# Holding the stationary operand over four segments and over two output halves in a fused attention and gMLP kernel

## The chip, the cores and the metric

The kernel runs on one core of a Trainium2 chip. The metric is the device time of one execution in microseconds.

## The reference

Two blocks with residuals over x of 2048 tokens by 1024 features: a segmented attention with memory (32 heads, 4 segments of 512 tokens), then a gMLP. The change touches only the gMLP:

```python
z  = gelu(einsum('bsd,df->bsf', x, w_in))            # 1024 -> 3584
z1 = z[..., :1792]                                   # the "first half": the first changed stage
z2 = layernorm(z[..., 1792:])
g  = einsum('ts,bsf->btf', w_sp, z2) + b_sp          # mixes tokens
return einsum('bsf,fd->bsd', z1 * g, w_out)          # output projection: the second changed stage
```

## The kernel before

Operations are recorded per engine and the waits are derived from what they read and write. A matmul computes `dst += lhs.T @ rhs`: `lhs` (128x128) is the stationary operand, loaded into the array by a weight load of its own, and `rhs` (here up to 512 columns) streams past it. The results gather in PSUM, of which the kernel uses eight banks; "evacuating" a bank is reading its result out. Every matmul call of this kernel makes a weight load and a matmul.

```python
def mm8(dst, lhs, rhs, n=8):                # one PSUM bank: n matmuls, n loads
    for i in range(n):
        pe.matmul(dst, lhs(i), rhs(i), start=(i == 0), stop=(i == n - 1))
# ... (attention; the second gMLP half; eight PSUM banks in turn from here on)

# first gMLP half: 14 output chunks fc, 4 segments s, 8 matmuls each
for k in range(4, 8):
    # ...
    for fl in range(w // 128):
        fc = lo // 128 + fl
        for s in range(NSEG):
            b = next_bank()
            mm8(bank(b), lambda i: WIN[k % 3][:, i, fl * 128:(fl + 1) * 128], lambda i: HNT[s][:, i, :])
            act.activation(Z1T[:, fc, s * 512:(s + 1) * 512], bank(b), ACTF.Gelu_apprx_tanh)
            if zq:
                z2_apply()
    # ... (loads of the next slabs)

for tb in range(4):
    # ... (token mixing: 14 banks of 16 matmuls into YT, evacuated by DVE)
    for tcl in range(4):                    # output projection: 16 chunks tc of 128 tokens
        tc = 4 * tb + tcl
        fin = FIN[tc % 3]
        sp.dma_start(fin[:], out2d[tc * 128:(tc + 1) * 128, :])
        for lo, w in ((0, 512), (512, 512)) if tc < NTC - 1 else ((0, 512), (512, 384), (896, 128)):
            b = next_bank()
            hs = slice(lo, lo + w)
            mm8(PS[:, b, 0:w], lambda i: YT[:, i, tcl * 128:(tcl + 1) * 128], lambda i: WOUT[:, i, hs], n=14)
            dve.tensor_tensor(fin[:, hs], fin[:, hs], PS[:, b, 0:w], ALU.add)
            sp.dma_start(out2d[tc * 128:(tc + 1) * 128, hs], fin[:, hs])
```

In the first half the stationary operand `WIN[.., i, ..]` does not depend on `s`, so it is loaded four times; in the output projection `YT[:, i, ..]` does not depend on the column half, so it is loaded twice.

The softmax here doesn't subtract the row's maximum and nothing guards it: scores larger than these inputs give would overflow.

## Time and profile before

| | before |
|---|---|
| time, median | 796.79 us (796.41 to 797.04, 3 runs) |
| span of the profiled run | 795.1 us |
| matmuls, weight loads | 5657, 5657 |
| PE busy, weight loads busy | 99%, 48% |
| first gMLP half | 405.6 to 502.3 us, 448 matmuls |
| output projection | four blocks between 550.9 and 793 us, 462 matmuls |
| start to start of the matmuls there, 512 columns | 215.8 ns |

The head of the profile's page, before. PE is TensorE's matmuls, PEld its weight loads (LDWEIGHTS), which overlap the matmuls, DVE is VectorE, ACT ScalarE, POOL GpSimd; the numbers are busy time, share of the span and count.

```profile
span 795.1 us, 13111 instructions
PE 789.9 (99%) x5657; PEld 378.4 (48%) x5657; DVE 379.3 (48%) x745; ACT 295.6 (37%) x347; POOL 172.1 (22%) x329
```

The groups of instructions of the changed stages, before: busy time in us and mean ns of one; after the second bar, idle time of the engine ahead of them.

```profile
L209 PE MATMUL ps<-w_out,yT 128*128 128x512 bf16 (+2 forms) x462 | 97.4, 373 | 0.0
L209 PE MATMUL ps<-hnT,win 128*128 128x512 bf16 x448 | 96.9, 379 | 0.0
L209 PEld LDWEIGHTS ps<-w_out,yT 128*128 128x128 bf16 x462 | 44.7, 98 | 52.3
L209 PEld LDWEIGHTS ps<-hnT,win 128*128 128x128 bf16 x448 | 43.8, 98 | 52.8
```

Two things are to be read here. A matmul's record lasts 379 ns, but 448 of them fill only 96.9 us: they overlap, and 96.9 us / 448 = 216 ns is the pace. And a load's 98 ns look like 45% of that pace. The starts of single instructions in the trace, from 410.142 us on, in ns (worked out from the trace's start times):

```text
410142 matmul   410144 load
410358 matmul   410360 load
410574 matmul   410576 load
```

Each load, for the next matmul, starts 1 or 2 ns after the start of the running one and ends 98 ns later, more than 100 ns before it is wanted. The starts also tell what is not streaming: 215.8 ns at 512 columns and 55.8 at 128 (in the last chunk) differ by 160 ns / 384 = 0.4167 ns per column, so 512 columns are 213.3 ns and 2.5 ns are left over. The windows of the changed stages, before (busy time of each engine in the window, count in brackets, then granted clock, DMA share, GB/s):

```profile
405.60:502.30 96.70, 96.70 (x450) 43.83 (x448) 10.88 (x21) 33.38 (x56) 5.65 (x15) 1.00 0.16 39
550.90:795.00 244.10, 241.90 (x1135) 110.34 (x1133) 81.67 (x119) 0.00 (x0) 0.00 (x0) 1.00 0.22 53
```

PE is busy for all of the first stage; ACT, which evacuates it, for a third.

### The profile page before, as it was taken

How to read it: one execution, taken by the hardware profiler on the slowest of the kernel's cores; microseconds unless marked ns; L12 is line 12 of the kernel's file. 1: busy time of each engine (PE TensorE's matmuls, PEld its weight loads, DVE VectorE, ACT ScalarE, POOL GpSimd, SP SyncE). 2: the span in 40 equal slices, each digit the busy share in tenths (PEclk: the TensorE clock that was granted, in tenths of full speed). 3: DMA queues.
4: the chain of work that ended last, by engine and by line, in shares of the span. 5: the costliest groups of instructions: out<-in, count | busy, mean ns of one | idle time of the engine just before them, and what ended most of it. 6: DMA issues, size and time to landing. Idle time of an engine off the chain costs nothing.

```text
span 795.1 us, 13111 instructions
## 1 busy us (share of the span) xinstructions
PE 789.9 (99%) x5657; PEld 378.4 (48%) x5657; DVE 379.3 (48%) x745; ACT 295.6 (37%) x347; POOL 172.1 (22%) x329
## 2 busy tenths in 40 slices
PE   8999999999999999999999999999999999999998
PEld 3445455554554455455544444444444444444444
DVE  7664689679854766744562000053234323323332
ACT  5777877887787675133333333100000000000000
POOL 4564565565553331100230000000000000000000
DMA  9862555363415325411116000740270043011002
GB/s 292 181 162 57 94 81 121 87 105 84 107 23 125 114 67 139 121 47 54 54 54 132 1 1 0 222 90 7 79 133 1 33 109 78 1 59 54 1 7 86
DMA packets 125002, 64.83 MB, mean 82 GB/s; under 512 B 94992, under 2 KB 113936, under 8 KB 124944
## 3 DMA queue, kind: packets, MB, share of 16 engines
q1 hardware_dynamic: 124944, 63.99, 33.7%
q8 instruction: 44, 0.72, 0.4%
q14 instruction: 14, 0.11, 0.1%
HBM read 32.51 MB, written 8.39 MB: 51 GB/s over the span
## 4 chain that ended last, share of the span: by engine, by line
PE 96%; DMA 2%; DVE 1%; ACT 0%; SPq 0%; issue 0%
PE ps L209 96%; DMA wq<-in_A_wq_dram 2%; DMA xch<-in_A_x_dram 0%; DVE stats L209 0%; ACT junk L209 0%; DVE xnT L209 0%; DVE lno L209 0%; SPq L209 0%; ACT xnT L209 0%; DVE mv L209 0%; DVE fin L209 0%
## 5 line engine op out<-in xcount | busy, mean ns | idle before, releaser
L209 PE MATMUL ps<-wspT,z 128*128 128x512 bf16 x896 | 194.0, 379 | 0.0
L209 ACT ACTIVATE e<-ps 128x2048 bf16<-128x2048 f32 (+1 forms) x96 | 152.6, 1590 | 41.9 <-PE ps L209 41.8
L209 PEld LDWEIGHTS ps<-wspT,z 128*128 128x128 bf16 x896 | 87.7, 98 | 105.7
L209 DVE TENSOR_TENSOR tmpg<-ps,brow 128x512 f32<-128x512 f32 x56 | 38.7, 691 | 196.7 <-DMA brow<-in_B_b_sp_dram 104.0
L209 POOL TENSOR_SCALAR_AFFINE_SELECT e<-e 128x512 bf16<-128x512 bf16 x128 | 90.4, 718 | 127.2 <-ACT e L209 127.1
L209 PE MATMUL ps<-win,hnT 128*128 128x448 bf16 x512 | 98.3, 352 | 0.0
L209 PE MATMUL ps<-w_out,yT 128*128 128x512 bf16 (+2 forms) x462 | 97.4, 373 | 0.0
L209 PE MATMUL ps<-hnT,win 128*128 128x512 bf16 x448 | 96.9, 379 | 0.0
L209 PEld LDWEIGHTS ps<-win,hnT 128*128 128x128 bf16 x512 | 49.7, 98 | 46.4 <-issue 0.2
L209 PEld LDWEIGHTS ps<-w_out,yT 128*128 128x128 bf16 x462 | 44.7, 98 | 52.3
L209 PEld LDWEIGHTS ps<-hnT,win 128*128 128x128 bf16 x448 | 43.8, 98 | 52.8
L209 PE MATMUL ps<-xnT,wk 128*128 128x512 bf16 x256 | 60.8, 380 | 0.0
L209 PE MATMUL ps<-xnT,wq 128*128 128x512 bf16 x256 | 60.6, 379 | 0.1
L209 PE MATMUL ps<-wv,xnT 128*128 128x512 bf16 x256 | 59.4, 380 | 0.2 <-ACT xnT L209 0.2
L209 ACT ACTIVATE z<-ps 128x448 bf16<-128x448 f32 x60 | 32.5, 543 | 69.4 <-PE ps L209 69.4
L209 PE MATMUL ps<-wo,oT 128*128 128x512 bf16 x256 | 58.0, 379 | 0.0
L209 ACT ACTIVATE z1T<-ps 128x512 bf16<-128x512 f32 x56 | 33.4, 597 | 63.3 <-PE ps L209 63.3
L209 DVE TENSOR_TENSOR fin<-fin,ps 128x512 bf16<-128x512 bf16 (+2 forms) x33 | 22.2, 671 | 71.2 <-DMA fin<-out_dram 39.7
L209 DVE BATCH_NORM_STATS2 zst<-z 128x6 f32<-128x448 bf16 x64 | 38.9, 619 | 30.1 <-ACT z L209 30.1
L209 PEld LDWEIGHTS ps<-v,e 128*128 128x128 bf16 x1280 | 38.8, 96 | 14.0 <-issue 6.5
L209 PE MATMUL ps<-v,e 128*128 128x33 bf16 x1280 | 42.2, 178 | 0.0
L209 DVE TENSOR_TENSOR yT<-tmpg,z1T 128x512 bf16<-128x512 f32 x56 | 38.8, 692 | 1.9
(86 smaller groups left out, 609.3 us busy)
## 6 DMA issues: line engine op xcount, KB each, us to landing
xch<-in_A_x_dram SPq DMA_DIRECT2D x16, 256.0 KB, 3.3
xr<-in_A_x_dram SPq DMA_DIRECT2D x16, 256.0 KB, 3.7
out_dram<-hch SPq DMA_DIRECT2D x16, 256.0 KB, 2.4
fin<-out_dram SPq DMA_DIRECT2D x16, 256.0 KB, 2.8
out_dram<-fin SPq DMA_DIRECT2D x31, 128.0 KB, 1.7
win<-in_B_w_in_dram SPq DMA_DIRECT2D x4, 896.0 KB, 5.1
w_out<-in_B_w_out_dram SPq DMA_DIRECT2D x1, 3584.0 KB, 12.7
win<-in_B_w_in_dram SPq DMA_DIRECT2D x3, 1024.0 KB, 5.2
```

The lines of the kernel that those rows point to most:

```text
L209: ins = getattr(e, op.name)(*op.args, **op.kw)
```

## The change

The intent: products with the same stationary operand run back to back and load it once. In the first half the four segments are computed together in four PSUM banks; in the output projection the two column halves in two banks (the last chunk, split in three parts, stays as it was). A held matmul is one that is issued without a weight load.

```diff
+def held_matmul(e, out, lhsT, rhs, start, stop):
+    return e.add_instruction(mybir.InstMatmult(
+        ..., tile_size=(128, 128), tile_position=(0, 0), ldweights=False,
+        ins=[e.lower_ap(rhs), e.lower_ap(lhsT)], outs=[e.lower_ap(out)]))
 ...
+    def mm_held(dsts, lhs, rhss, n):
+        for i in range(n):
+            for k, (d, r) in enumerate(zip(dsts, rhss)):
+                (pe.matmul_held if k else pe.matmul)(d, lhs(i), r(i), start=(i == 0), stop=(i == n - 1))
 ...
+            bs = [next_bank() for _ in range(NSEG)]
+            mm_held([bank(b) for b in bs], lambda i: WIN[k % 3][:, i, fl * 128:(fl + 1) * 128],
+                    [lambda i, s=s: HNT[s][:, i, :] for s in range(NSEG)], 8)
             for s in range(NSEG):
-                b = next_bank()
-                mm8(bank(b), lambda i: WIN[k % 3][:, i, fl * 128:(fl + 1) * 128], lambda i: HNT[s][:, i, :])
-                act.activation(Z1T[:, fc, s * 512:(s + 1) * 512], bank(b), ACTF.Gelu_apprx_tanh)
+                act.activation(Z1T[:, fc, s * 512:(s + 1) * 512], bank(bs[s]), ACTF.Gelu_apprx_tanh)
 ...
+            parts = ((0, 512), (512, 512)) if tc < NTC - 1 else ((0, 512), (512, 384), (896, 128))
+            bs = [next_bank() for _ in parts]
+            if tc < NTC - 1:
+                mm_held([bank(b) for b in bs], lambda i: YT[:, i, tcl * 128:(tcl + 1) * 128],
+                        [lambda i, lo=lo, w=w: WOUT[:, i, lo:lo + w] for lo, w in parts], 14)
+            for (lo, w), b in zip(parts, bs):
 ... (additions and stores as before, now after both halves)
```

("..." marks what is left out.)

More of the change, by code (lines that the diff above doesn't have):

```diff
@@ L26 @@
 GRAN = 32
+def held_matmul(e, out, lhsT, rhs, start, stop):
+    return e.add_instruction(mybir.InstMatmult(
+        name=e.bass.get_next_instruction_name(), engine=mybir.EngineType.PE, start_tensor_calc=start,
+        stop_tensor_calc=stop, tile_size=(128, 128), tile_position=(0, 0), ldweights=False,
+        ins=[e.lower_ap(rhs), e.lower_ap(lhsT)], outs=[e.lower_ap(out)]))
 class _Op:
@@ L208, in run @@
                     e.wait_ge(o.dma if o.dma is not None else sems[o.eng], o.val)
-                ins = getattr(e, op.name)(*op.args, **op.kw)
+                if op.name == "matmul_held":
+                    ins = held_matmul(e, *op.args, **op.kw)
+                else:
+                    ins = getattr(e, op.name)(*op.args, **op.kw)
                 if op.dma is not None:
@@ L912, in bass_sequential_preLN__memory_aug_infini_attn__mixer_gmlp__prompt_kernel @@
             sp.dma_start(fin[:], out2d[tc * 128:(tc + 1) * 128, :])
-            for lo, w in ((0, 512), (512, 512)) if tc < NTC - 1 else ((0, 512), (512, 384), (896, 128)):
-                b = next_bank()
+            parts = ((0, 512), (512, 512)) if tc < NTC - 1 else ((0, 512), (512, 384), (896, 128))
[4 more added lines that the diff above has]
+            for (lo, w), b in zip(parts, bs):
                 hs = slice(lo, lo + w)
-                mm8(PS[:, b, 0:w], lambda i: YT[:, i, tcl * 128:(tcl + 1) * 128], lambda i: WOUT[:, i, hs], n=14)
+                if tc == NTC - 1:
+                    mm8(PS[:, b, 0:w], lambda i: YT[:, i, tcl * 128:(tcl + 1) * 128], lambda i: WOUT[:, i, hs], n=14)
                 dve.tensor_tensor(fin[:, hs], fin[:, hs], PS[:, b, 0:w], ALU.add)
```

## The prediction

> **What bounds the kernel.** TensorE. The page gives PE 99% of a 795.1 us span, the chain of waits 96% PE, and the list of waits shows PE waiting for other engines only 2.7 us in all, none of it after 400 us, where both changed stages lie. The granted clock is 1.000.
>
> **The two stages.** By the windows, the first gMLP half runs from 405.6 to 502.3 us (448 matmuls, 128x512) and the output projection (462 matmuls) is spread in four blocks over 550.9 to 793 us. Every matmul has its own weight load (5657 of each); one load takes 98 ns. In the trace, start to start of the matmuls in both stages is 215.8 ns, while the load of the next operand starts 2 ns after each matmul's start. 512 columns at 2.4 GHz are 213.3 ns, so 2.5 ns per matmul are not streaming. The Trainium skill (TensorE: Matmul & The Clock Gate, "Step-by-step") says that loads are pulled ahead of running matmuls into a background buffer; this trace agrees. The same page ("Wait — 56ns, not 53.3ns?") calls the 2.5 ns a fixed cost per matmul; the trace agrees that it is fixed: 448 columns take 189.2 ns (186.7 + 2.5) and 128 columns 55.8 ns (53.3 + 2.5).
>
> **What the change does.** It removes 336 weight loads (three of four in 448) and 210 (15 chunks x 14), 546 in all: 53.5 us of weight-load busy time, all of it under running matmuls, so none of it on the critical path. It moves evacuations: four gelus (0.60 us each) now come in a burst after 32 matmuls (6.9 us), on banks 0-3 and 4-7 in turn; the burst (about 2.4 us) has 6.9 us. In the output projection two additions (0.69 us) follow 28 matmuls (6.04 us); also free. Alternating banks costs nothing where the kernel already does it (the early V projection: 216 ns).
>
> **On the critical path.** Only the 2.5 ns could go, if it were the change of weights and not the matmul itself: 546 x 2.5 ns = 1.4 us at most, 0.2%. I think it more likely (about 60 to 40) that it stays. At the tail, both additions of the chunk before the last now come after its 28 matmuls, so the last load of fin is issued about 0.7 us later. Before, 0.73 us of idle time followed the addition that waits for that load (790.63 us); the shift just fits: 0 to 0.2 us.
>
> **Prediction.** 796.3 us, 8 in 10 between 794.8 and 797.4. Faster by over 2%: 1%; within 2%: 98%; slower by over 2%: 1%.
>
> **What would show it.** Weight loads 5111, PEld busy 378 down to about 325 us, about 41% of the span; PE busy still 99%; start to start of held matmuls 215.8 ns (or 213.3 if the swap was the cost); no new PE waits in the two stages; the first half's window still 96.7 us (95.9 if the swap was the cost); DVE no longer waiting on fin in the output projection.
>
> **What would make it wrong.** A held matmul that costs more than one with its own load (for instance, a load after held matmuls that is not pulled ahead: up to 98 ns x 322 loads (112 + 210) = 32 us, 4% slower); a lower granted clock; a semaphore wait that now falls on the first matmul of a group of four banks.

## The result, and the profile after

| | before | after |
|---|---|---|
| time, median | 796.91 us (796.41 to 797.15, 4 runs, one more than above) | 796.97 us (796.54 to 797.23, 4 runs) |
| ratio | | 1.0001, 95% interval 0.9984 to 1.0018 |
| weight loads | 5657 | 5111 |
| weight loads busy | 378.4 us | 325.6 us |
| span of the profiled run | 795.1 us | 795.2 us |

A ratio here and below is the mean time of one kernel's fast runs over that of the other's fast runs of the same rounds, so it is not quite the ratio of the medians. The time did not move.

The head of the page, after, and the groups of the changed stages. L31 is the line of the held matmul.

```profile
span 795.2 us, 12473 instructions
PE 785.4 (99%) x5565; PEld 325.6 (41%) x5111; DVE 378.1 (48%) x745; ACT 291.0 (37%) x347; POOL 173.5 (22%) x329
...
L31 PE MATMUL ps<-hnT,win 128*128 128x512 bf16 x332 | 90.6, 379 | 0.5
L220 PE MATMUL ps<-w_out,yT 128*128 128x512 bf16 (+2 forms) x243 | 82.4, 367 | 0.0
L31 PE MATMUL ps<-w_out,yT 128*128 128x512 bf16 x210 | 79.6, 379 | 0.5
...
L220 PEld LDWEIGHTS ps<-w_out,yT 128*128 128x128 bf16 x252 | 24.2, 98 | 72.2 <-issue 69.1
...
L220 PEld LDWEIGHTS ps<-hnT,win 128*128 128x128 bf16 x112 | 11.0, 98 | 85.0 <-issue 84.9
```

The loads went as meant: 448 to 112 and 462 to 252. The 92 matmuls that seem to be gone (5565 of 5657) are missing records, not missing work: in the first half the start times are 215 or 216 ns apart but for eight gaps of 431 or 432 ns, twice that, each where one record is missing; token mixing has 18 such gaps and the output projection nine. With those set aside the pace is 215.8 ns, as before, for held matmuls and for those with a load. The load of the next operand starts 1 or 2 ns after the start of the last held matmul of a group (matmul at 410.891 us, load at 410.892). The windows, after:

```profile
405.60:502.30 96.70, 96.22 (x441) 11.00 (x113) 10.94 (x21) 27.51 (x54) 5.71 (x15) 1.00 0.17 38
550.90:795.00 244.10, 240.84 (x1114) 89.82 (x923) 80.13 (x119) 0.00 (x0) 0.00 (x0) 1.00 0.22 53
```

In the first window PEld fell from 43.83 to 11.00 us, while the stage is as long as it was: 96.48 us from the start of its first matmul to that of its last (405.83 to 502.30 before, 405.93 to 502.40 after; after, the first record is missing, and its start is set one step before the second's). The output projection takes 241.71 us by the same measure, before and after.

ACT's 5.9 us less in that window are not work saved in the stage's bottleneck. 1.3 us of them are evacuations that now fall behind the window's end (ACT has 1.94 us in the window after it, 0.60 before); the other 4.5 come from the new order. The evacuations in order of time, before and after (start in us, length, instruction, idle time ahead of it and what ended it):

```profile
488.91 0.60 ACT L209 ACTIVATE z1T<-ps 128x512 bf16<-128x512 f32 x1 [1.13 <-PE ps L209]
490.63 0.60 ACT L209 ACTIVATE z1T<-ps 128x512 bf16<-128x512 f32 x1 [1.13 <-PE ps L209]
492.36 0.60 ACT L209 ACTIVATE z1T<-ps 128x512 bf16<-128x512 f32 x1 [1.13 <-PE ps L209]
494.09 0.60 ACT L209 ACTIVATE z1T<-ps 128x512 bf16<-128x512 f32 x1 [1.13 <-PE ps L209]
```

```profile
488.36 2.06 ACT L220 ACTIVATE z1T<-ps 128x512 bf16<-128x512 f32 x4 [4.84 <-PE ps L220]
495.27 2.06 ACT L220 ACTIVATE z1T<-ps 128x512 bf16<-128x512 f32 x4 [4.84 <-PE ps L220]
```

Four gelus in a row overlap and take 2.06 us, not four times 0.60 us. ACT waits for PE in both kernels, so this gains nothing.

The tail, before and after: DVE's last additions, and the queue's issue of the last load of fin (the buffer with the rows of the output to which a product is added).

```profile
787.90 0.38 SPq L209 DMA_DIRECT2D fin<-out_dram  x1
790.63 0.69 DVE L209 TENSOR_TENSOR fin<-fin,ps 128x512 bf16<-128x512 bf16 x1 [3.19 <-DMA fin<-out_dram]
792.05 0.55 DVE L209 TENSOR_TENSOR fin<-fin,ps 128x384 bf16<-128x384 bf16 x1 [0.73 <-PE ps L209]
792.83 0.29 DVE L209 TENSOR_TENSOR fin<-fin,ps 128x128 bf16<-128x128 bf16 x1 [0.23 <-PE ps L209]
```

```profile
788.46 0.38 SPq L220 DMA_DIRECT2D fin<-out_dram  x1
791.32 1.39 DVE L220 TENSOR_TENSOR fin<-fin,ps 128x512 bf16<-128x512 bf16 x2 [3.32 <-DMA fin<-out_dram]
792.93 0.29 DVE L220 TENSOR_TENSOR fin<-fin,ps 128x128 bf16<-128x128 bf16 x1 [0.23 <-PE ps L220]
```

The load is issued 0.56 us later and the addition that waits for it starts 0.69 us later. It runs into the next one (the "x2" of 1.39 us), which had 0.73 us of idle time ahead of it before; the last addition still starts 0.23 us after DVE fell idle, released by PE. The delay was swallowed whole. The 0.10 us between the two last lines was there already when the last matmul started (792.577 us before, 792.678 after), and already at the first matmul of the second gMLP half, ahead of both changed stages (291.837 and 291.938).

### The profile page after: what moved, and what is told of

It is laid out like the page before. It is cut to its first block, busy times and chain, and to the rows that moved or that the text cites. A ratio compares the mean times of both kernels' runs of the same rounds, so it can differ in the third digit from the quotient of the medians.

```text
span 795.2 us, 12473 instructions
## 1 busy us (share of the span) xinstructions
PE 785.4 (99%) x5565; PEld 325.6 (41%) x5111; DVE 378.1 (48%) x745; ACT 291.0 (37%) x347; POOL 173.5 (22%) x329
## 4 chain that ended last, share of the span: by engine, by line
PE 94%; DVE 5%; issue 1%; ACT 0%; DVEq 0%
PE ps L220 79%; PE ps L31 15%; DVE stats L220 1%; DVE hch L220 1%; DVE otok L220 0%; DVE lno L220 0%; DVE pqk L220 0%; DVE ta L220 0%; ACT e L220 0%; DVE etmp L220 0%; DVE rd L220 0%; DVE mv L220 0%; DVE rdm L220 0%; DVE upd L220 0%; DVE xnT L220 0%
## 5 line engine op out<-in xcount | busy, mean ns | idle before, releaser
L31 PE MATMUL ps<-hnT,win 128*128 128x512 bf16 x332 | 90.6, 379 | 0.5
L220 PE MATMUL ps<-w_out,yT 128*128 128x512 bf16 (+2 forms) x243 | 82.4, 367 | 0.0
L31 PE MATMUL ps<-w_out,yT 128*128 128x512 bf16 x210 | 79.6, 379 | 0.5
L220 PE MATMUL ps<-xnT,wq 128*128 128x512 bf16 x225 | 53.9, 379 | 1.8 <-issue 0.2
L220 ACT ACTIVATE z1T<-ps 128x512 bf16<-128x512 f32 x56 | 28.9, 603 | 68.7 <-PE ps L220 68.7
L220 PEld LDWEIGHTS ps<-w_out,yT 128*128 128x128 bf16 x252 | 24.2, 98 | 72.2 <-issue 69.1
L220 PEld LDWEIGHTS ps<-hnT,win 128*128 128x128 bf16 x112 | 11.0, 98 | 85.0 <-issue 84.9
```

What stands on the lines that cost most here:

```text
L31: return e.add_instruction(mybir.InstMatmult(name=e.bass.get_next_instruction_name(), engine=mybir.EngineType.PE, start_tensor_calc=start, ...
L220: ins = getattr(e, op.name)(*op.args, **op.kw)
```

## The experiments

The theory: loads are wholly hidden under the matmuls, and the 2.5 ns by which a matmul of 512 columns exceeds its 213.3 ns of streaming belong to the matmul. Two rivals also give an unchanged time: the loads saved did gain and the new order of banks and evacuations cost as much (rival 1), or one stage gained and the other lost (rival 2). The first four runs shared a chip, and 7 runs of the kernel before (median 796.69 us).

### order_only: the new order with every load

```diff
-                (pe.matmul_held if k else pe.matmul)(d, lhs(i), r(i), start=(i == 0), stop=(i == n - 1))
+                pe.matmul(d, lhs(i), r(i), start=(i == 0), stop=(i == n - 1))
```

> The new order of matmuls and evacuations, but every matmul with its own weight load (5657 loads). Theory (loads are wholly hidden, and the 2.5 ns over streaming belong to the matmul, not to the load): start to start 215.8 ns in both stages, the time of before within 0.1%, ratio 1.000. Rival 1 (the removed loads gained up to 546 x 2.5 ns = 1.4 us and the new order of banks and evacuations costs as much): this kernel pays the order without the gain, about 798.3 us, ratio about 1.002, with a start to start above 216 or a wait of PE in one of the two stages.

Measured: 796.56 us, ratio 0.9997 (0.9982 to 1.0012), 5657 loads, start to start 215.8 ns in both stages, and no wait of PE in either. The bursts of four gelus in 2.06 us are there too, so ACT's saved time comes from the order and not from the loads. The order costs nothing; rival 1 falls.

### z1_only and out_only: one half of the change each

```diff
 z1_only: the output projection is that of the kernel before
-            if tc < NTC - 1:
-                mm_held([bank(b) for b in bs], ... 14)
+                mm8(PS[:, b, 0:w], ... n=14)
 out_only: the first gMLP half is that of the kernel before
-            mm_held([bank(b) for b in bs], ... 8)
+                mm8(bank(b), ...)
```

> Only the first gMLP half holds its operand (336 loads fewer: 5321). Theory: ratio 1.000, window of that stage 96.7 us, held matmuls 215.8 ns apart. Rival 2 (one half of the change gains and the other loses): this one is faster by about 0.8 us (336 x 2.5 ns), window 95.9 us, and out_only slower by as much, or the other way round.

> Only the output projection holds its operand (210 loads fewer: 5447). Theory: ratio 1.000, held matmuls 215.8 ns apart, the last load of fin issued about 0.6 us later than before and nothing lost at the end. Rival 2: a difference of 0.5 us or more with the sign opposite to z1_only.

Measured: z1_only 796.64 us, ratio 0.9997 (0.9982 to 1.0012), 5321 loads; out_only 796.59 us, ratio 0.9998 (0.9981 to 1.0014), 5447 loads. Neither half differs from before, in time or in pace (215.8 ns), and rival 2 falls. By the intervals alone a gain of 0.19% (1.5 us) could hide, more than rival 2 asks for; the traces are the finer evidence. From the start of its first matmul to that of its last, the output projection takes 241.71 us and the first half 96.48 us in before, after, order_only, z1_only, out_only and hold_all alike, so neither rival has room for a gain and a loss that cancel.

### hold_all: half of all loads taken away (wrong results on purpose)

```diff
     def mm8(dst, lhs, rhs, n=8):
         for i in range(n):
-            pe.matmul(dst, lhs(i), rhs(i), start=(i == 0), stop=(i == n - 1))
+            (pe.matmul_held if i else pe.matmul)(dst, lhs(i), rhs(i), start=(i == 0), stop=(i == n - 1))
 (and in mm_held: held if k or i)
```

> Wrong results on purpose: in every product of the helper that computes one output bank (Q and K projections, attention output, second gMLP half, token mixing, output projection) and in the changed stages, only the first matmul of a group loads its operand; all others run on what was loaded, about 2830 loads fewer (about 2830 left), so about half of PEld's busy time goes. Theory: start to start still 215.8 ns at 512 columns and 189.2 ns at 448, ratio 1.000 (within 0.1%). If the 2.5 ns were the swap of operands: 7 us faster (ratio 0.991), 213.3 and 186.7 ns. If loads tax the kernel in any other way (reads, queue), some gain between.

Measured: 796.88 us, ratio 1.0001 (0.9986 to 1.0016); the results are wrong, as meant. The head of its page and its window of the first half:

```profile
span 795.0 us, 10280 instructions
PE 790.2 (99%) x5657; PEld 107.4 (14%) x2826; DVE 377.9 (48%) x745; ACT 291.1 (37%) x347; POOL 172.3 (22%) x329
```

```profile
405.60:502.30 96.70, 96.70 (x450) 1.39 (x15) 10.85 (x21) 27.64 (x54) 5.61 (x15) 1.00 0.17 38
```

With 2831 loads and 271 us of load time gone, five times what the change took away, nothing moved: the window has the same 450 matmuls in the same 96.70 us with 15 loads as with 448. The pace is 215.8 ns at 512 columns and 189.2 at 448 (the second gMLP half), as before. If the 2.5 ns were the change of operands, this kernel would be 7 us faster (2831 x 2.5 ns).

### many_loads: how many loads fit under one matmul

Redundant loads of the same operand are put ahead of each matmul of the first half, their number by output chunk.

```diff
+                loads = {4: 2, 5: 3, 6: 4, 7: 6, 8: 8, 9: 12, 10: 16}.get(fc, 1)
+                # matmul_xN: N - 1 plain weight loads of lhsT, then the matmul with its own
+                    getattr(pe, "matmul_x%d" % loads)(bank(b), WIN[...], HNT[s][:, i, :], ...)
```

> The kernel before, with redundant weight loads of the same operand ahead of each 128x512 matmul of the first gMLP half: by output chunk 1, 1, 1, 1, 2, 3, 4, 6, 8, 12, 16, 1, 1, 1 loads per matmul (32 matmuls each). Measures how many loads fit under one matmul. Theory A (loads stream into the array at the pace seen in attention, where 33-column matmuls with a load each start 25 ns apart, so about 25 ns each): 215.8 ns at 1 to 8 loads, above it from 9 on: about 300 ns at 12 and 400 ns at 16. Theory B (each load holds the loading path for the 98 ns that its record lasts): 215.8 ns at 2, about 294 at 3, 392 at 4, 588 at 6, 784 at 8, 1176 at 12, 1568 at 16. Theory C (only one load ahead fits, a second one has to wait for the running matmul to end): already 2 loads cost, by about 100 ns or more.

Measured (824.48 us, ratio 1.0349, results correct), start to start of the matmuls, from the trace:

| loads per matmul | 1 | 2 | 3 | 4 | 6 | 8 | 12 | 16 |
|---|---|---|---|---|---|---|---|---|
| ns | 215.8 | 215.8 | 215.8 | 215.8 | 216.6 | 296.7 | 456.7 | 616.7 |

Theory B (98 ns each) and C (one load ahead) fall. Theory A was right that several fit, but its 25 ns per load was not: from 8 loads on, each further load adds (616.7 - 296.7) / 8 = 40.0 ns. Two windows of this run, of 4 and of 8 loads per matmul:

```profile
447.00:452.00 5.00, 5.00 (x25) 5.00 (x94) 0.00 (x0) 1.79 (x3) 0.00 (x0) 1.00 0.00 0
461.00:469.50 8.50, 8.50 (x30) 8.50 (x231) 0.00 (x0) 2.39 (x4) 0.00 (x0) 1.00 0.01 2
```

Both show PEld busy for the whole window, yet the first loses nothing and the second 81 ns per matmul: a load's record lasts 98 ns, but loads in a row start 40 ns apart, several in flight at once. "Busy" here means a load was under way, not that the path was full. (The 16-load value is from the first three steps of that stretch; then the granted clock fell to 0.50, and the later starts, 726.7 ns apart, are taken up under loads_narrow.)

### pieces: narrower matmuls, with own loads and held

The 512 columns of a matmul are cut into pieces with the same stationary operand; held means one load and then pieces without.

```diff
+                pw, hold = {6: (256, 0), 7: (256, 1), 8: (128, 0), 9: (128, 1), 10: (64, 0), 11: (64, 1),
+                            12: (32, 0), 13: (32, 1)}.get(fc, (512, 0))
+                for i in range(8):
+                    for p in range(0, 512, pw):
+                        (pe.matmul_held if hold and p else pe.matmul)(
+                            PS[:, b, p:p + pw], WIN[...], HNT[s][:, i, p:p + pw], ...)
```

> The kernel before, with the 512 columns of a matmul of the first gMLP half cut into narrower matmuls of the same operand, by output chunk: 256 columns with own loads, 256 held, 128 own, 128 held, 64 own, 64 held, 32 own, 32 held (held: one load, then the rest without). Asks from which width a load would cost. Theory: start to start is columns/2.4 + 2.5 ns with or without loads at 256, 128 and 64 (109.2, 55.8, 29.2 ns), since 33 columns with a load each already start 25 ns apart in attention; at 32 both are 25 ns if a floor of the matmul itself binds (then holding gains nowhere here), and the held one is about 16 ns if the 25 ns are the load. If held is shorter at 128 or 64 already, the load costs earlier than the kernel's own lines show.

Measured (810.72 us, ratio 1.0176, results correct), start to start:

| columns | 256 | 128 | 64 | 32 |
|---|---|---|---|---|
| own load, ns | 109.2 | 55.8 | 29.2 | 25.0 |
| held, ns | 109.2 | 55.8 | 29.2 | 25.0 |

The windows of 32 columns, own loads and then held (PE, PEld):

```profile
491.00:497.00 6.00, 6.00 (x247) 6.00 (x244) 0.00 (x0) 0.86 (x2) 0.00 (x0) 1.00 0.02 5
504.00:514.00 10.00, 10.00 (x407) 2.38 (x25) 0.00 (x0) 2.04 (x4) 0.00 (x0) 1.00 0.02 3
```

247 matmuls in 6 us and 407 in 10 us are the same pace, with 244 loads and with 25. Holding gains nothing at any width, not even where a load's record is four times as long as the step from matmul to matmul. The extra 2.5 ns are there with and without loads at 256, 128 and 64 columns: they belong to the matmul.

### loads_narrow: does the 40 ns depend on the width?

```diff
+                loads, pw = {4: (5, 512), 5: (7, 512), 6: (2, 128), 7: (3, 128), 8: (2, 64), 9: (1, 32),
+                             10: (2, 32), 11: (3, 32)}.get(fc, (1, 512))
```

> The kernel before with redundant loads, by output chunk of the first gMLP half: 512 columns 5 loads, 512 columns 7 loads, 128 columns 2 loads, 128 columns 3 loads, 64 columns 2 loads, 32 columns 1 load, 32 columns 2, 32 columns 3, others as before. many_loads gave 216.7, 296.7 and 456.8 ns at 6, 8 and 12 loads, which is 40 ns for each load beyond the first, plus 16.7 ns. If that line holds whatever the width: 215.8, 256.7, 56.7 (128 columns, 2 loads: just above its 55.8), 96.7, 56.7, 25, 56.7, 96.7 ns. Rival (it is the number of loads that wait behind a long matmul, and with short ones they pass at 25 ns each): 128 columns with 2 and 3 loads 55.8 and 75, 64 columns with 2 loads 50, 32 columns 25, 50, 75.

Measured (904.9 us, ratio 1.1358, results correct): 512 columns with 5 loads 215.8 ns, with 7 loads 256.7; 128 columns with 2 loads 57.8, with 3 loads 96.7; 64 columns with 2 loads 57.8; 32 columns with 1 load 25.0, with 2 loads 57.8 (23 steps in a row, until the granted clock fell to 0.50 at 497.6 us). At full clock the line "40 ns for each load beyond the first, plus 16.7 ns" holds at 512, 128, 64 and 32 columns wherever it is longer than the matmul itself, within 1.1 ns; the rival (25 ns each with short matmuls) would have given 75 where 96.7 was measured, and 50 where 57.8 was, at 64 and at 32 columns.

At the clock of 0.50 the starts at 32 columns are 73.3 ns apart with 2 loads and 120.0 with 3, and in many_loads 726.7 with 16 at 512 columns: 46.7 ns for each further load (120.0 - 73.3, and (726.7 - 120.0) / 13). A matmul of 512 columns with one load went from 215.8 to 426.7 ns there. So the matmul's pace halves with the granted clock, while a load's step grows only from 40.0 to 46.7 ns. Why is not settled: the runs do not show whether the step is that of the array's loading path or of the issue of the load instruction.

### after_4banks and before_4banks: what the new order needs

The burst of gelus was predicted free because it has 6.9 us until its banks are wanted. Here both kernels have only four of the eight banks in the first half.

```diff
+    rot["banks"], rot["n"] = [0, 1, 2, 3], 0
     for k in range(4, 8):
 ...
+    rot["banks"], rot["n"] = [4, 5, 6, 7, 0, 1, 2, 3], 0     # all eight again, from token mixing on
```

> The changed kernel with only four PSUM banks in turn in the first gMLP half, so that each group of four segments has to wait for the burst of gelus of the group before (0.52 us apart in a burst, the first starting about 0.65 us before the group's last matmul is through). My theory of why the burst was free (it had eight banks, so a whole group's 6.9 us) says: now it costs, the last of the four gelus ending about 1.7 us after the group's last matmul has started and its bank wanted 0.65 us after, so about 1.0 to 1.3 us per group, 13 times, 13 to 17 us in all: ratio 1.017 to 1.021, PE waiting for ACT in this stage. Rival (the evacuations have slack enough in any order): ratio 1.000.

> The kernel before with four banks in turn in the same stage: each bank is wanted again only 5.2 us after its group is through, and its gelu takes 0.6 us, so no cost but perhaps a wait of under 1 us at the entry into the stage: ratio 1.000 to 1.001.

Measured: after_4banks 810.37 us, ratio 1.0174 (1.0158 to 1.0189); before_4banks 796.72 us, ratio 1.0000 (0.9983 to 1.0016). So the changed order lost 13.7 us with four banks and the old order nothing. The loss in order of time, in after_4banks, around the border of two groups:

```profile
427.99 2.06 ACT L220 ACTIVATE z1T<-ps 128x512 bf16<-128x512 f32 x4 [5.86 <-PE ps L220]
428.64 0.10 PEld L220 LDWEIGHTS ps<-hnT,win 128*128 128x128 bf16 x1 [1.18 <-ACT z1T L220]
```

The load of the next group starts only after the first gelu (427.99 + 0.60). The next three matmuls each wait for one more gelu: their starts are 484, 490 and 490 ns apart, and the one before 421, instead of 216. That is 1.02 us per group, 13 times 13.3 us, and 0.6 us at the entry of the stage. My expectation named 13 to 17 us, and a wait of PE for ACT; the list of PE's waits shows only the 0.6 us at the entry. The reason is the matmul's record of 379 ns, which covers most of a step of 490 ns, so PE looks busy, and the list leaves out the 100 ns or so that remain of each; PEld's idle time and the distances of the starts show the stall. A little of my reasoning for the size was off as well: I had the burst end 1.7 us after the start of the group's last matmul, and it was 1.8 us (427.99 + 2.06 - 428.22).

## Why the prediction was right

- **The bound.** TensorE, with 215.8 ns per matmul of 512 columns, in both kernels and all variants at full clock with up to 5 loads per matmul, but for the stalls of after_4banks. Right.
- **No new waits.** The list of PE's waits after 400 us is empty in both kernels, as predicted.
- **The loads removed.** 546 fewer, 5111 left, PEld busy 325.6 us: as predicted. They were called off the critical path because each starts 1 or 2 ns after the matmul before it and is over in 98 ns; hold_all shows it on a scale five times larger, and many_loads shows that four loads per matmul still cost nothing. The Trainium skill (TensorE: Matmul & The Clock Gate, "Step-by-step") explains the hiding with loads pulled ahead into a background buffer; the starts in the trace agree with it.
- **The 2.5 ns.** The prediction left open, at 60 to 40, whether they belong to the matmul or to the change of operand. They belong to the matmul: held and unheld are the same at 512, 448, 256, 128 and 64 columns. So the 1.4 us at most did not come, and the 0.5 us by which 796.3 lay below the 796.79 us of before weighed a gain that does not exist. This is the term that was mis-sized; measured it is 0. Both outcomes lay within the stated range, and the runs of one kernel spread over 0.7 to 1.0 us, so the total time could not have told them apart: the starts did.
- **The evacuations.** Free, as predicted, because there are eight banks; with four they cost 13.7 us. The gelus were costed at 2.4 us a burst and took 2.06.
- **The tail.** The load of fin was expected 0.7 us later; it was issued 0.56 us later and its addition came 0.69 us later (0.10 us of both is the offset that was there before the changed stages); the end did not move. Right.
- **DVE waiting on fin.** Predicted gone in the output projection; mostly right: from 39.7 us in 12 waits to 8.1 us in 2, by the list of DVE's waits.
- **What could have made it wrong** did not occur: loads after held matmuls are pulled ahead (1 or 2 ns after the last one's start), the granted clock stayed at 1.000, and no wait fell on the first matmul of a group.

## What to carry to other kernels

Before removing weight loads, look at the starts of matmuls and loads in order of time, not at the loads' busy time: if a load starts with the running matmul and the matmuls keep their pace, removing loads buys nothing, and here that held from 512 down to 32 columns. Holding an operand over several banks is not free in itself: it gathers the evacuations in bursts, and with no spare set of banks that cost 1.7%. Where matmul records overlap, judge a stall by the distances of their starts, since "busy" hides it.

## What the Trainium skill lacked or had wrong

- Perfetto Trace Analysis, "Identifying the Most-Contended Engine", recommends the busy share of weight loads, beside the share of peak FLOP/s, as a measure of TensorE's distance to roofline. Here that share went from 48% to 41% (the change) and 14% (hold_all), and the time stayed at 797 us; in many_loads it was 100% of a window with no loss at 4 loads per matmul and with 81 ns lost per matmul at 8.
- TensorE: Matmul & The Clock Gate, "LDWEIGHTS (loading the stationary operand)", gives a load as its columns / 1.2 ns, by which an estimate for 128 columns is 107 ns. The records show 98 ns, and the section does not say that loads overlap each other: they start 40 ns apart in a row, and a load with each matmul of 32 columns fits into steps of 25.0 ns.
- The same page, "Back-to-back issue gap", gives streams of loads and matmuls about 131 ns per matmul at 512 columns and 81 ns at 128. Here they ran at 215.8 and 55.8 ns; its formula for the isolated matmul (columns / 2.4 + 2.5) fits every width from 64 to 512.
- The same page, "Wait — 56ns, not 53.3ns?", calls the 2.5 ns fixed per matmul, but does not say whether a matmul without a load pays it. It does: 215.8, 109.2, 55.8 and 29.2 ns, held or not.
- I found no page that told how many loads one matmul hides, nor how the step from load to load follows the granted clock. Here 5 loads cost nothing at 512 columns, a sixth 0.8 ns (216.6), and each further one 40 ns; at a granted clock of 0.50 the step was 46.7 ns.
